# Attention, capacity routing and a cos-MLP on one core: scores in halves of the array's rows, and the float64 pieces moved

## The chip, the cores and the metric

The kernel runs on one core of a Trainium2 chip. The metric is the time of one execution on the device in microseconds (us). Three runs of the kernel before gave a median of 1265.24 us (1261.33 to 1281.06).

## The reference

Three layers follow one another; the output is 1792 x 768 in float32.

```
q_n, k_n = rmsnorm(q, g_q), rmsnorm(k, g_k)          # 4 batches, 12 heads, 448 rows, 64 columns
scores = q_n @ k_n.T / 8;  attn = softmax(scores);  x = attn @ v        # x: 1792 x 768
logits = x @ w_gate                                  # 8 experts, each takes at most 224 tokens
walk over the logits in falling order, give each token to the first expert that has room
out[of e] = relu(x[of e] @ w1[e]) @ w2[e]            # 768 -> 1024 -> 768
h = out @ w_in;  y = (h * cos(h)) @ w_out            # 768 -> 2048 -> 768, w_in and w_out in float64
```

The order of the logits decides which token goes where, so products are kept close to float32: an operand is cut into a high and a low part in the float32r type, and three products (high x high, high x low, low x high) stand for one. The float64 matrices arrive as pairs of 32-bit words and are turned into such parts on the chip.

## The kernel before

The program consists of two plans. A plan (`class Plan`, L51) records each operation with what it reads and writes; `run` (L161) then lists the operations engine by engine, with costs from a table (`cost`, L64) and due times, and that order is fixed in the program. On each engine a step starts in that order. Steps without a successor, as those of the float64 pieces, have the latest due times and fill what is free.

The first plan holds attention and the router's start. Attention goes by pairs of heads, 24 of them (`for P_ in range(NPR)`). For one pair:

- `front` and `turn` (L434) normalise q and k, transpose them with TensorE and cut them into hi and lo parts. For each head these are copied by DMA (`copy`, L366, SP's queue) into a key tile `TK` and a query tile `QS`, so that hi and lo of one head stand on top of each other in the 128 partitions, and a second half `[:, 1]` holds the hi part with one more row: ones for the keys, minus the row maxima for the queries.
- `shifts` (L484) finds the row maxima that keep the exponential in range: seven products s of 128 query rows with all keys, each reduced by VectorE (cm), a transpose, a sign change (cr), and a copy of the row into `QS`. `shift` (L502) does it for the first pair, head by head.
- `scores` (L535) makes, for each of four groups of 112 keys and each head, a score tile in one of two PSUM banks (st): one product over 128 rows (hi and lo of the keys with hi of the queries) and one over 65 rows (hi of the keys with lo of the queries, and the shift). ScalarE writes its exponential to a buffer pf, of which there are `NPF` = 12.
- `weigh` (L553) multiplies the exponentials with v (po: two heads in column halves of the array, float32, two instructions each) and with ones (dn: the sums, in column quarters).
- `rows` (L579) adds the gate logits to the sums' bank by one float32 product of the weighted values with `wg` (32 columns out, 448 columns in), and transposes both by small products with `pick`; VectorE takes the reciprocals of the sums. `tail` (L597) transposes the weighted values for x.

Beside it runs `Narrow.plan` (L254): each of 56 pieces (32 of w_in with 128 x 384 elements, 24 of w_out with 128 x 512) is loaded by SP (nr), turned by ScalarE and VectorE (na, then nr again), and written back to memory by SP. `EARLY` = 36 pieces belong to the first plan, the rest to the second.

The second plan (`moe`) takes the experts in four groups of two. For each expert the router's `phase` picks the next expert and its tokens; for each group the two experts follow, then the cos-MLP on both. The first three phases are the quick ones (`quick`, with count products into rt). The MLP of the first group reads parts that the late pieces have written.

Of the kernel before, what the change touches and what calls it, by code (L numbers as in the profile page):

```python
# [25 lines left out]
class Step:  # L26
    __slots__ = ("ways", "after", "before", "late", "wait", "ready", "end", "eng", "dma", "start", "rush")
# [23 lines left out]
class Plan:  # L51
# [4 lines left out]
    def __init__(self, nc):  # L56
        self.nc, self.steps, self.seen, self.group, self.rush = nc, [], {}, None, 0.0
        self.shared, self.ahead, self.beside = True, 0.0, False
        self.tensor = Engine(self, "PE", nc.tensor)
        self.vector = Engine(self, "DVE", nc.vector)  # L60
        self.scalar = Engine(self, "ACT", nc.scalar)
        self.gpsimd = Engine(self, "POOL", nc.gpsimd)

    def cost(self, eng, name, out, r, kw):  # L64
        n = max([out.free_size()] + [x.free_size() for x in r])
        if eng == "PE":
            if self.key(out)[1]:
                return 0.055
            rhs = r[1] if name == "matmul" else r[0]
            passes = 1 if rhs.dtype != F32 else 4 if name == "matmul" else 2  # L70
            if name == "matmul" and rhs.dtype == F32 and self.beside:
                passes *= {32: 0.32, 64: 0.6}.get(out.partition_size(), 1)
            return max(out.free_size() / 2333.0 + 0.011, 0.107 if rhs.dtype == F32R else 0.0467) * passes
# [28 lines left out]
    def add(self, ways, reads, writes, dma=None):  # L102

        if self.group is not None:
            self.group.append((ways[0], reads, writes))
            return
        s = Step(ways, dma)
        s.rush = self.rush + self.ahead * (ways[0][0] != "DVE")
# [52 lines left out]
    def run(self, order, prefer=0.0, edge=1.0, lag=2.6, hold=0.7, by=6.0, queue=9e9, more=0.0):  # L161
# [21 lines left out]
        free, bus = {}, 0.0  # L183
# [3 lines left out]
        while avail:  # L187
            best = None
            for e in ("PE", "DVE", "ACT", "POOL", "SP"):
# [16 lines left out]
                c = min((g for g in good if g[0] <= t0 + 0.02), key=lambda g: (g[1].late, idx[g[1]]))  # L206
                ahead = [g for g in good if c[0] < g[0] < c[0] + c[2][1] * hold and g[1].late < c[1].late - by]
                if ahead:
                    c = min(ahead, key=lambda g: (g[1].late, idx[g[1]]))
# [19 lines left out]

LEAST = float(np.array([0x38000000], np.uint32).view(np.float32)[0])  # L230
# [53 lines left out]
EPS = 1e-9  # L284
TUNE_A = (3.5, 0.3, 4.5, 0.7, 30.0, 1.2)
NPF = 12
# [8 lines left out]
NHL = 3  # L295
# [15 lines left out]
def attention(tc, P, R, ident, q, k, v, g_q, g_k, w_gate, x_dram, L, other):  # L311
# [4 lines left out]
    with ExitStack() as ctx:  # L316
# [8 lines left out]
        TK = [cst.tile([128, 2, S], F32R, name=f"tk{i}") for i in range(8)]  # L325
        QS = [cst.tile([128, 2, 2, S], F32R, name=f"qs{i}") for i in range(4)]
# [12 lines left out]
        hls = ring("hl", NHL, [128, 2, S], F32R)  # L339
        his = ring("kh", 4, [128, S], F32R)  # L340
        los = ring("kl", 2, [128, S], F32R)
# [59 lines left out]
        for t in TK:  # L401
            zset(t[D:D + 1, 1], 1.0)
# [31 lines left out]
        def turn(P_, i, rs, j):  # L434

            if True:
# [10 lines left out]
                if i:  # L447
                    hi, lo = keys[P_], _ = his(), los()
                else:
                    hl = hls()  # L450
                    hi, lo = hl[:, 0], hl[:, 1]
                if P_ == 0:
                    o = TK[0][0:D, 0] if i else QS[0][0:D, 0, 0]
                    sc.activation(o, p[0:D, :S], AF.Copy, scale=gs[0:D] if i else 1.0)
                if i:
                    sc.activation(hi, p[:, :S], AF.Copy, scale=gs)
                    ve.scalar_tensor_tensor(lo, p[:, :S], gs, hi.bitcast(F32), op0=ALU.mult, op1=ALU.subtract)
                else:
                    sc.activation(hi, p[:, :S], AF.Copy)
                    ve.tensor_tensor(lo, p[:, :S], hi.bitcast(F32), op=ALU.subtract)  # L460
                for h in range(2):
                    r = slice(h * D, (h + 1) * D)
                    if P_ == 0 and h == 0:
                        if i:
                            copy(TK[0][0:D, 1], hi[r])
                            copy(TK[0][D:128, 0], lo[r])
                        else:
                            copy(QS[0][D:128, 0, 0], hl[r, 0])
                            copy(QS[0][0:D, 1, 0], hl[r, 1])
                    elif i:  # L470
                        t = TK[(2 * P_ + h) % 8]
                        copy(t[0:D], hi[r].unsqueeze(1).to_broadcast([D, 2, S]))
                        copy(t[D:128, 0], lo[r])
                    else:
                        t = QS[P_ % 4]
                        copy(t[D:128, 0, h], hl[r, 0])
                        copy(t[0:D, :, h], hl[r])
                    if P_ and not i:
                        z = slice(S - D, S) if h == 0 else slice(0, D)
                        P.either("tensor_copy", mix[P_ % 4][r, r], hi[r, z])  # L480

        keys = {}

        def shifts(P_):  # L484


            cm, t, x = cms(), QS[P_ % 4], 7
            for m in range(x):
                p = b1()[:, :S]
                if m == 3:  # L490
                    w, y = mix[P_ % 4], keys.pop(P_)
# [8 lines left out]
            copy(t[D:D + 1, 1].rearrange("o j s -> o (j s)").rearrange("o (m p) -> o m p", p=128), cr)  # L500

        def shift(P_, heads=(0, 1)):  # L502

            cm, t = cms()[0:CP], QS[P_ % 4]
            K = D if P_ == 0 and heads[0] == 0 else 128
            for h in heads:
                for c in range(NC):
                    p = b1()[0:CP, :S]
                    pe.matmul(p, t[0:K, 0, h, c * CP:(c + 1) * CP], TK[(2 * P_ + h) % 8][0:K, 0], start=True, stop=True)
                    ve.tensor_reduce(cm[:, h * NC + c:h * NC + c + 1], p, AX.X, ALU.max)  # L510
            n, o = len(heads) * NC, heads[0] * NC
            p = bt()[0:n, 0:CP]
            pe.transpose(p, cm[:, o:o + n], ident[0:CP, 0:CP])
            cr = crs()[0:n, 0:CP]
            sc.activation(cr, p, AF.Copy, scale=-1.0)
            row = t[D:D + 1, 1, heads[0]:heads[-1] + 1]
            copy(row.rearrange("o j (c p) -> o (j c) p", c=NC), cr)
# [17 lines left out]
        def scores(P_, a, z):  # L535

            qs = QS[P_ % 4]
            for c in range(a, z):
                sl = slice(c * CP, (c + 1) * CP)
                for h in range(2):  # L540
                    p, tk = bs()[0:CP, :S], TK[(2 * P_ + h) % 8]
# [5 lines left out]
                    block(both)  # L547
                    pf = exps[P_, h, c] = pfs()
                    sc.activation(pf[0:CP], p, AF.Exp)
# [3 lines left out]
        def weigh(P_):  # L553
# [5 lines left out]
            for c in range(NC):  # L559
                def both():  # L560
                    for h in range(2):
                        pe.matmul(po[h * D:(h + 1) * D], t[:, h, c], exps[P_, h, c][0:CP], start=c == 0, stop=c == NC - 1)
# [4 lines left out]
            for h in range(2):  # L567
                def four():
                    for c in range(NC):
                        n = CP + (c == 0)  # L570
                        pe.matmul(pd[32 * c:32 * c + 32], ones[0:n, h], exps.pop((P_, h, c))[0:n], start=h == 0,
                                  stop=h == 1 and c > 0)

                block(four)
# [4 lines left out]
        def rows(y):  # L579
# [3 lines left out]
            block(lambda: pe.matmul(pd[0:32], wg[:, y % NP], outs[y], start=False, stop=True))  # L583
# [3 lines left out]
            for c in range(NC):  # L587
                pe.matmul(p[:, c, 0:18], dn[:, c * CP:(c + 1) * CP], pick[:, 0:18], start=True, stop=True)
# [77 lines left out]
        for P_ in range(min(NPR, AHEAD)):  # L666
# [4 lines left out]
            if P_ == 0:  # L671
                shift(0, (0,))
                shift(0, (1,))
# [20 lines left out]
        P.run(zip(chain, chain[1:]), *TUNE_A)  # L694
# [604 lines left out]
EARLY = 36  # L1299
# [63 lines left out]
```

## Time and profile before

| what | value |
|---|---|
| median of three runs | 1265.24 us |
| the profiled execution: its own time, its span | 1270.09 us, 1268.3 us |
| TensorE, VectorE, ScalarE busy, of the span | 93%, 69%, 52% |
| granted TensorE clock, mean | 0.952 |

The names in the rows: PE is TensorE's products, PEld its weight loads, DVE VectorE, ACT ScalarE, POOL GpSimd, SP the engine whose queue issues most transfers. `st<-qs,tk` is a product that writes a score tile from a query and a key tile; buffer numbers are left out. L47 is the line of the recording helper, so nearly all operations bear it, and the tile names tell them apart. In the timeline, durations of neighbours overlap, because an engine starts the next instruction before the last one has ended; the distance between starts is the cost in a row of instructions. TensorE runs a float32 product as two instructions and a float32r product as one.

### The profile page before, as it was taken

Reading aid. Unit: us, or ns where it says so; the run is one execution under the profiler, and the core shown is the slowest. Engines: PE = TensorE matmul, PEld = TensorE weight load, DVE = VectorE, ACT = ScalarE, POOL = GpSimd, SP = SyncE. Lnnn points to the kernel's source line nnn. Section 1 sums busy time; section 2 is a strip of 40 time slices with the busy share of each in tenths; the row PEclk is TensorE's granted clock in tenths of the full one; section 3 lists DMA queues with packets and bytes.
Section 4 is the critical chain, followed back from the end, with each engine's and each line's share of the span. In section 5 each row is a group of like instructions: output and inputs, shape, how many; then the busy total and the mean of one; then the engine's idle time right before and its main releaser. Section 6 shows DMA issues by size and latency. Waiting matters only on the chain.

```text
span 1268.3 us, 20996 instructions
## 1 busy us (share of the span) xinstructions
PE 1185.7 (93%) x7247; PEld 957.8 (76%) x7247; DVE 873.0 (69%) x2511; ACT 663.8 (52%) x1574; POOL 97.4 (8%) x150
## 2 busy tenths in 40 slices
PE   6999999999985989999789989899999999999996
PEld 4555555555533889788679978789998888999996
DVE  6778768888869878996586569457648737646501
ACT  5577677665654545762454458154538434535500
POOL 4211111111000000000002000000100000100001
PEclk9999899999975789999889999999999999999998
DMA  8888869889754569888867766855776783766762
GB/s 212 193 211 217 207 173 251 227 246 257 232 199 138 154 192 301 282 279 288 288 207 212 216 201 227 239 189 162 225 207 214 234 266 113 223 206 221 244 205 71
DMA packets 201548, 273.52 MB, mean 216 GB/s; under 512 B 16193, under 2 KB 177250, under 8 KB 195298
## 3 DMA queue, kind: packets, MB, share of 16 engines
q1 hardware_dynamic: 198882, 261.17, 69.1%
q0 software_dynamic: 2560, 11.01, 2.9%
q8 instruction: 57, 0.93, 0.3%
q14 instruction: 49, 0.40, 0.1%
HBM read 202.79 MB, written 36.46 MB: 189 GB/s over the span
## 4 chain that ended last, share of the span: by engine, by line
PE 39%; DVE 6%; DMA 6%; ACT 1%; issue 0%; SPq 0%; POOL 0%; POOLq 0%; DVEq 0%; ACTq 0%
PE acc L47 37%; DMA ws<-in_moe_w_dram 2%; DMA AB<-rows 2%; DVE r L47 2%; PE tr L47 1%; DMA wx<-w_in 1%; DVE oh L47 1%; ACT oh L47 1%; PE rt L47 1%; DVE gl L47 1%; DMA nr<-in_moe_w_out_dram 0%; DVE S L47 0%; POOL out_dram L1272 0%; DVE xe L47 0%; DVE ind L47 0%
## 5 line engine op out<-in xcount | busy, mean ns | idle before, releaser
L47 PE MATMUL acc<-gh,wx 128*128 128x224 f32 (+1 forms) x1952 | 376.9, 318 | 0.0
L47 PEld LDWEIGHTS acc<-gh,wx 128*128 128x128 f32 x1952 | 287.3, 195 | 21.3 <-issue 8.6
L47 PE MATMUL acc<-x2h,wx 128*128 128x448 f32 x768 | 228.0, 373 | 0.0
L47 DVE TENSOR_TENSOR wx<-ws,wx 128x768 fp32r<-128x768 f32 (+1 forms) x112 | 119.9, 1070 | 67.0 <-ACT wx L1183 66.8
L47 PEld LDWEIGHTS acc<-x2h,wx 128*128 128x128 f32 x768 | 146.2, 190 | 18.0 <-issue 6.4
L1183 ACT ACTIVATE wx<-ws 128x768 fp32r<-128x768 f32 (+1 forms) x109 | 102.2, 939 | 104.3 <-PE acc L47 73.1
L47 PE MATMUL acc<-gl,wx 128*128 128x448 f32 (+1 forms) x400 | 147.8, 370 | 0.0
L47 PE MATMUL acc<-x2l,wx 128*128 128x448 f32 x384 | 141.6, 369 | 0.0
L47 PE MATMUL acc<-xe,wx 128*128 128x224 f32 x1152 | 136.5, 280 | 0.1
L47 PEld LDWEIGHTS acc<-xe,wx 128*128 128x128 f32 x1152 | 134.5, 196 | 0.5 <-DVE wx L47 0.3
L47 DVE TENSOR_REDUCE cm<-s 128x1 f32<-128x448 f32 (+1 forms) x169 | 99.3, 616 | 43.2 <-PE s L47 42.2
L47 ACT ACTIVATE pf<-st 112x448 f32<-112x448 f32 x192 | 96.0, 540 | 54.8 <-PE st L47 51.4
L47 ACT ACTIVATE oh<-oh 128x896 bf16<-128x896 bf16 x80 | 75.3, 942 | 81.6 <-DVE oh L47 81.5
L47 PE MATMUL st<-qs,tk 128*112 128x448 f32 (+1 forms) x384 | 108.0, 396 | 8.7 <-DMA qs<-cr 7.8
L47 ACT ACTIVATE r<-r 128x448 f32<-128x448 f32 x128 | 73.4, 575 | 42.4 <-DVE r L47 40.9
L47 PE MATMUL po<-pf,vr 112*64 112x448 f32 x384 | 89.7, 580 | 0.0
L47 PEld LDWEIGHTS st<-qs,tk 128*112 128x112 f32 (+1 forms) x384 | 64.1, 182 | 32.1 <-DMA qs<-cr 9.9
L47 DVE TENSOR_SCALAR oh<-AB,b 128x896 bf16<-128x896 f32 x80 | 51.6, 682 | 50.8 <-DMA AB<-rows 50.1
L47 PEld LDWEIGHTS acc<-gl,wx 128*128 128x128 f32 x400 | 78.6, 196 | 5.5
L47 PEld LDWEIGHTS acc<-x2l,wx 128*128 128x128 f32 x384 | 73.0, 190 | 5.3
L1144 POOL DMA_INDIRECT xr<-x,idx x16 | 16.5, 1034 | 694.7 <-issue 215.7
L47 ACT ACTIVATE sq<-qk 112x64 f32<-112x64 f32 (+1 forms) x195 | 57.8, 302 | 20.7 <-DMA qk<-in_q_dram 6.3
(235 smaller groups left out, 1668.7 us busy)
## 6 DMA issues: line engine op xcount, KB each, us to landing
wx<-w_in SPq DMA_DIRECT2D x64, 768.0 KB
wx<-w_out SPq DMA_DIRECT2D x48, 1024.0 KB
ws<-in_moe_w_dram SPq DMA_DIRECT2D x64, 384.0 KB
ws<-in_moe_w_dram SPq DMA_DIRECT2D x48, 512.0 KB
nr<-in_moe_w_in_dram SPq DMA_DIRECT2D x32, 384.0 KB
w_in<-nr SPq DMA_DIRECT2D x32, 384.0 KB
nr<-in_moe_w_out_dram SPq DMA_DIRECT2D x24, 512.0 KB
w_out<-nr SPq DMA_DIRECT2D x24, 512.0 KB
```

Source lines behind the costliest of these rows:

```text
L47: self.plan.add([(self.eng, self.plan.cost(self.eng, name, out, r, kw), lambda: f(*args, **kw))], r, w)
L1144: P.add([("POOL", 1.03, lambda x=x, h=h: nc.gpsimd.indirect_dma_start(out=x, out_offset=None, in_=x_rows, in_offset=bass.IndirectOffsetOnA ...
L1183: P.add([("ACT", 0.093 + n * 0.1067, lambda: nc.scalar.activation(hi, s, AF.Copy)), ("DVE", 0.07 + n * 0.0667, lambda: nc.vector.tensor_co ...
```

## The change

Keys and queries of a pair stay as they leave the transpose, both heads beside each other in the upper and lower 64 partitions, hi and lo in two halves of one tile; the copies go. A score block is made for both heads at once, in four rounds: in each, two products over 64 rows, one for each head, in the upper and the lower half of the array's rows, into the two st banks. The fourth round adds the shift, by a product of a matrix `heads` (a row of ones for each head) with a tile `shift_rows`. `shifts` takes the maxima from the same tiles and serves the first pair too; `shift` goes. The gate product in `rows` is replaced by four products with 18 columns out, which add to the pick products. po is made in two blocks of eight instructions, dn in one. The planner learns the tile form of a product, counts `SWITCH` for a change of form and prefers the form that stands (`SAME`). pf has 18 buffers. `EARLY` is 56: all pieces belong to the first plan.

```diff
-    def run(self, order, prefer=0.0, edge=1.0, lag=2.6, hold=0.7, by=6.0, queue=9e9, more=0.0):
+    def run(self, order, prefer=0.0, edge=1.0, lag=2.6, hold=0.7, by=6.0, queue=9e9, more=0.0,
+            same=0.0):
...
+                def first(g):
+                    return g[1].late - same * (e == "PE" and g[1].mode == mode), idx[g[1]]
...
+            if w[0] == "PE":
+                st += SWITCH * (s.mode != mode)
+                mode = s.mode
...
-NPF = 12
+NPF = 18
...
-        TK = [cst.tile([128, 2, S], F32R, name=f"tk{i}") for i in range(8)]
-        QS = [cst.tile([128, 2, 2, S], F32R, name=f"qs{i}") for i in range(4)]
+        keys = [cst.tile([128, 2, S], F32R, name=f"kk{i}") for i in range(NKQ)]
+        queries = [cst.tile([128, 2, S], F32R, name=f"qq{i}") for i in range(NKQ)]
+        shift_rows = [cst.tile([128, 512], F32R, name=f"sr{i}") for i in range(4)]
+        heads = cst.tile([128, CP], F32R, name="heads")
...
-            for m in range(x):
+            k, q = keys[P_ % NKQ], queries[P_ % NKQ]
+            for m in (0, 4, 1, 5, 2, 6, 3):
                 p = b1()[:, :S]
...
-                    w, y = t[:, 0, h, c:c + 128], TK[(2 * P_ + h) % 8][:, 0]
+                    r = slice(h * D, (h + 1) * D)
+                    w, y = q[r, 0, c:c + 128], k[r, 0]
...
+            for h in range(2):
+                copy(t[h * D:h * D + 1].rearrange("o (m p) -> o m p", p=128), cr[3 * h:3 * h + 4])
...
+                ps = [bs()[0:CP, :S] for h in range(2)]
+
+                def both():
+                    for j in range(4):
+                        for h in range(2):
+                            r = slice(h * D, (h + 1) * D)
+                            w = heads[r] if j == 3 else k[r, j == 1, sl]
+                            y = t[r, h * D:h * D + S] if j == 3 else q[r, int(j == 2)]
+                            pe.matmul(ps[h], w, y, start=j == 0, stop=j == 3)
...
-                    def both():
-                        pe.matmul(p, tk[:, 0, sl], qs[:, 0, h], start=True, stop=False)
-                        pe.matmul(p, tk[0:D + 1, 1, sl], qs[0:D + 1, 1, h], start=False, stop=True)
...
-            block(lambda: pe.matmul(pd[0:32], wg[:, y % NP], outs[y], start=False, stop=True))
...
-                pe.matmul(p[:, c, 0:18], dn[:, c * CP:(c + 1) * CP], pick[:, 0:18], start=True, stop=True)
+                pe.matmul(p[:, c, 0:18], dn[:, sl], pick[:, 0:18], start=True, stop=False)
+                pe.matmul(p[:, c, 0:18], outs[y][:, sl], wg[:, y % NP, 0:18], start=False, stop=True)
...
-EARLY = 36
+EARLY = 56
```

On TensorE, in the middle of attention, the order before reads as follows (st is a score tile, s a product for the maxima, t a transpose, dn with wg the gate product):

```order
L47 MATMUL s_219<-tk_147,qs_152 128x448
L47 MATMUL s_218<-tk_147,qs_152 128x448
L47 MATMUL t_217<-ident,qn_170 128x112 x4
L47 MATMUL st_220<-qs_151,tk_145 112x448 x2
L47 MATMUL st_221<-qs_151,tk_146 112x448 x2
L47 MATMUL dn_223<-xe_203,wg 32x448
L47 MATMUL s_219<-kh_179,mx_185 128x448
```

At a like place the order after reads:

```order
L47 MATMUL st_220<-qq_150,kk_145 112x448
L47 MATMUL st_221<-qq_150,kk_145 112x448
L47 MATMUL st_220<-qq_150,kk_145 112x448
L47 MATMUL st_221<-qq_150,kk_145 112x448
L47 MATMUL st_220<-qq_150,kk_145 112x448
L47 MATMUL st_221<-qq_150,kk_145 112x448
L47 MATMUL st_220<-sr_151,heads 112x448
L47 MATMUL st_221<-sr_151,heads 112x448
L47 MATMUL s_218<-kk_141,qq_146 128x448
L47 MATMUL t_216<-pick,dn_208 112x18
L47 MATMUL t_216<-wg,xe_205 112x18
```

Both st banks are now taken by one block of eight products, a product for the maxima stands alone behind it, and the gate product has become small ones between the pick products.

On VectorE, at the end of attention, the order before has these rows from the last reciprocal on (na and nr are a float64 piece, L and m the router's first steps):

```order
L47 RECIPROCAL r_214<-t_217 112x8
L47 SCALAR_TENSOR_TENSOR na_228<-nr_226,na_228 128x512
L47 TENSOR_TENSOR part<-t_217,r_214 112x4x2x8
L47 TENSOR_SCALAR na_229<-na_229 128x512
L47 TENSOR_REDUCE L<-part 112x32
L47 TENSOR_SCALAR na_229<-na_229 128x512
L47 TENSOR_REDUCE m<-L 112x4
L47 SCALAR_TENSOR_TENSOR na_228<-nr_226,na_228 128x512
```

The order after has, from its last reciprocal on:

```order
L47 RECIPROCAL r_214<-t_216 112x8
L47 TENSOR_TENSOR part<-t_216,r_214 112x4x2x8
L47 TENSOR_REDUCE L<-part 112x32
L47 TENSOR_REDUCE m<-L 112x4
L47 TENSOR_TENSOR oe<-L,m 112x32
```

The pieces have left this place; the last of the 56 now ends ahead of the 23rd reciprocal, and the others stand between the pairs from the first one on (before: two pieces by the third reciprocal, 34 by the 24th; after: six and 56).

## Rows read from the trace of the kernel before

**Rows 1.** The page: the span, and two engines' busy time, share and instructions.

```profile
span 1268.3 us, 20996 instructions
PE 1185.7 (93%) x7247; PEld 957.8 (76%) x7247; DVE 873.0 (69%) x2511; ACT 663.8 (52%) x1574; POOL 97.4 (8%) x150
```

**Rows 2.** Windows: stretch, length, then busy us (instructions) of PE, PEld, DVE, ACT, POOL; clock, DMA.

```profile
25.00:359.00 334.00, 324.72 (x1880) 179.61 (x1878) 266.82 (x746) 220.40 (x694) 46.61 (x42) 0.98 0.83 222
...
377.00:417.00 40.00, 20.09 (x109) 14.70 (x110) 36.07 (x209) 15.97 (x49) 2.29 (x4) 0.53 0.47 142
...
502.00:731.00 229.00, 215.51 (x1322) 195.31 (x1322) 169.08 (x488) 116.08 (x223) 9.88 (x12) 0.96 0.78 256
731.00:939.00 208.00, 200.30 (x1257) 184.36 (x1256) 132.24 (x349) 102.99 (x195) 9.14 (x12) 0.98 0.68 205
939.00:1141.00 202.00, 196.42 (x1256) 181.62 (x1255) 129.54 (x340) 103.14 (x196) 9.14 (x12) 0.99 0.69 211
```

**Rows 3.** Tile t, the reciprocals: duration ns min/median/max, first and last start us.

```profile
L47 DVE RECIPROCAL r<-t x24: 194/200/209, 59.0 to 376.5; 112x8 f32<-112x8 f32 x24
```

**Rows 4.** Timeline of PE within one pair: start us, us, instruction.

```profile
205.46 0.94 PE L47 MATMUL dn<-xe,wg 128*32 128x448 f32 x2
206.33 0.47 PE L47 MATMUL s<-kh,mx 128*128 128x448 f32 x1
206.64 0.37 PE L47 MATMUL s<-tk,qs 128*128 128x448 f32 x1
206.84 0.97 PE L47 MATMUL st<-qs,tk 128*112 128x448 f32 x4
207.65 0.87 PE L47 MATMUL t<-pick,dn 128*112 128x18 f32 x8
208.37 0.66 PE L47 MATMUL s<-tk,qs 128*128 128x448 f32 x2
208.86 0.98 PE L47 MATMUL st<-qs,tk 128*112 128x448 f32 x4
209.77 0.97 PE L47 MATMUL po<-pf,vr 112*64 112x448 f32 x4
210.67 0.28 PE L47 MATMUL t<-ident,cm 128*7 128x128 f32 x1
...
211.27 2.48 PE L47 MATMUL po<-pf,vr 112*64 112x448 f32 x12
213.67 0.47 PE L47 MATMUL s<-tk,qs 128*128 128x448 f32 x1
```

**Rows 5.** Timeline of PE at the start of attention, with the wait before each.

```profile
26.93 0.46 PE L47 MATMUL st<-qs,tk 65*112 65x448 f32 x1 [1.14 <-DMA qs<-cr]
...
36.26 0.46 PE L47 MATMUL st<-qs,tk 65*112 65x448 f32 x1 [2.25 <-DMA qs<-cr]
```

**Rows 6.** Timeline of DVE at the end of attention.

```profile
376.66 0.69 DVE L47 SCALAR_TENSOR_TENSOR na<-nr,na 128x512 int32<-128x512 int32 x1
377.27 0.26 DVE L47 TENSOR_TENSOR part<-t,r 112x64 f32<-112x64 f32 x1
377.41 0.42 DVE L47 TENSOR_SCALAR na<-na 128x512 f32<-128x512 f32 x1
377.74 0.25 DVE L47 TENSOR_REDUCE L<-part 112x32 f32<-112x96 f32 x1
```

**Rows 7.** Groups by form: count, busy us, mean ns of one, idle before.

```profile
L47 DVE SCALAR_TENSOR_TENSOR na<-nr,na 128x384 int32<-128x384 int32 x64 | 35.4, 583 | 0.1
L47 DVE SCALAR_TENSOR_TENSOR na<-nr,na 128x512 int32<-128x512 int32 x48 | 32.6, 685 | 0.1
...
L47 ACT ACTIVATE pf<-st 112x448 f32<-112x448 f32 x192 | 96.0, 540 | 54.8 <-PE st L47 51.4 <-PE dn L47 2.6
```

**Rows 8.** Timeline of PE behind attention's last products, with the wait before it.

```profile
382.82 0.94 PE L47 MATMUL dn<-ab 112*128 112x128 bf16 x4 [6.66 <-DVE ab L47]
```

**Rows 9.** Groups by form of PE from 502 to 731 us: the quick route's count products.

```profile
L47 PE MATMUL rt<-AB 112*128 112x128 bf16 x32 | 5.6, 225 | 1.1 <-ACT AB L47 0.6
...
L47 PE MATMUL rt<-AB 112*128 112x64 bf16 x16 | 2.7, 200 | 0.3
```

More of the change, by code (lines that the diff above doesn't have):

```diff
@@ L26 @@
 class Step:
-    __slots__ = ("ways", "after", "before", "late", "wait", "ready", "end", "eng", "dma", "start", "rush")
+    __slots__ = ("ways", "after", "before", "late", "wait", "ready", "end", "eng", "dma", "start", "rush", "mode")
     def __init__(self, ways, dma):
@@ L57, in __init__ @@
         self.nc, self.steps, self.seen, self.group, self.rush = nc, [], {}, None, 0.0
-        self.shared, self.ahead, self.beside = True, 0.0, False
+        self.shared, self.ahead, self.beside, self.halves = True, 0.0, False, False
         self.tensor = Engine(self, "PE", nc.tensor)
@@ L107, in add @@
         s = Step(ways, dma)
+        s.mode = None
+        if ways[0][0] == "PE" and isinstance(reads[0], bass.AP):
+            w = reads[0]
+            s.mode = (w.partition_size() <= D, 32 if w.free_size() <= 32 else 64 if w.free_size() <= 64 else 128)
         s.rush = self.rush + self.ahead * (ways[0][0] != "DVE")
@@ L182, in run @@
             s.late -= s.rush
-        free, bus = {}, 0.0
+        free, bus, mode = {}, 0.0, None
         avail = [s for s in self.steps if s.wait == 0]
@@ L205, in run @@
                 t0 = min(g[0] for g in good)
-                c = min((g for g in good if g[0] <= t0 + 0.02), key=lambda g: (g[1].late, idx[g[1]]))
-                ahead = [g for g in good if c[0] < g[0] < c[0] + c[2][1] * hold and g[1].late < c[1].late - by]
+                def first(g):
+                    return g[1].late - same * (e == "PE" and g[1].mode == mode), idx[g[1]]
+                c = min((g for g in good if g[0] <= t0 + 0.02), key=first)
+                ahead = [g for g in good if c[0] < g[0] < c[0] + c[2][1] * hold and first(g)[0] < first(c)[0] - by]
                 if ahead:
-                    c = min(ahead, key=lambda g: (g[1].late, idx[g[1]]))
+                    c = min(ahead, key=first)
                 if best is None or c[0] < best[0]:
@@ L400, in attention @@
                 wg[r, :, c], w_gate.rearrange("(e h d) n -> h d e n", h=2, d=D)[h]))], [], [wg[r, :, c]], dma=0.1)
-        for t in TK:
-            zset(t[D:D + 1, 1], 1.0)
+        for t in shift_rows + [heads]:
+            zset(t, 0.0)
+        for h in range(2):
+            zset(heads[h * D:h * D + 1], 1.0)
         zset(ones, 0.0)
@@ L499, in shifts @@
             sc.activation(cr, p, AF.Copy, scale=-1.0)
[L500 to L517, printed above, removed]
+            t = shift_rows[P_ % 4]
+            for h in range(2):
+                copy(t[h * D:h * D + 1].rearrange("o (m p) -> o m p", p=128), cr[3 * h:3 * h + 4])
         vals = {}
@@ L566, in weigh, with fours @@
             P.beside = True
-            for h in range(2):
-                def four():
+            def fours():
+                for h in range(2):
                     for c in range(NC):
                         n = CP + (c == 0)
-                        pe.matmul(pd[32 * c:32 * c + 32], ones[0:n, h], exps.pop((P_, h, c))[0:n], start=h == 0,
-                                  stop=h == 1 and c > 0)
-                block(four)
+                        pe.matmul(pd[32 * c:32 * c + 32], ones[0:n, h], exps.pop((P_, h, c))[0:n], start=h == 0, stop=h == 1)
+            block(fours)
             P.beside = False
@@ L693, in attention @@
         other(P, cst)
-        P.run(zip(chain, chain[1:]), *TUNE_A)
+        P.run(zip(chain, chain[1:]), *TUNE_A, same=SAME)
 CP, NCOL, E, CAP = 112, 16, 8, 224
```

71 lines of the change are left out of this document (26 added, 45 removed).

## Prediction

> **What bounds the kernel now.** I read the page first [rows 1]: TensorE is busy for 93% of the span, VectorE for 69%. Such a mean says nothing about a program with two parts, so next come the stretches [rows 2]. In the attention part, 25 to 359 us, TensorE is busy 324.7 of 334 us and VectorE 266.8; the first is the bound and the second has 67 us to spare. From 377 to 417 us the router runs alone: TensorE is busy half of the time, VectorE 36 of 40. After that TensorE has over 93% in each stretch. The three stretches 502:731, 731:939 and 939:1141 each hold one cos-MLP of a group and the two experts of the next, and take 229, 208 and 202 us: the first, in which the 20 late float64 pieces are turned into parts, is 21 to 27 us longer.
>
> The pace of attention: one reciprocal ends each of the 24 pairs of heads, the first at 59.0, the last at 376.5 us [rows 3]; the mean distance is (376.5 - 59.0) / 23 = 13.8 us. To see what fills a pair I read TensorE's timeline from start to start [rows 4], since the durations overlap. Four score products (st) take 0.81 and 0.91 us; sixteen make 3.5 us a pair. Products for the row maxima (s) take 0.20 to 0.31 us each; the gate product with wg 0.87 us, the eight pick products 0.72 us. For po, four instructions take 0.90 and twelve 2.40 us, hence 0.375 us for one couple of 64-column halves and 0.15 us for leaving that form: 0.90 - 2 x 0.375. A wait plays hardly any part here.
>
> **The change, step by step.** The sum is made against the profiled execution: span 1268.3, own time 1270.1 us, that is 4.9 us above the median of the runs shown (1265.2). I work out a difference and take 4.9 us off at the end.
>
> (a) Scores. Before, a score tile is two products over 128 and 65 rows; after, one block is four rounds of two products over 64 rows, each head in its half of the rows. The columns streamed are the same if both halves run together. No row shows two row halves at once. The nearest row is po: its column halves run together, one couple in 0.375 us, where the gate product without a partner takes 0.87 us for its two instructions [rows 4]. The ends for a round are therefore 0.205 us (a single score product, 0.81 / 4) and 0.41 us (no overlap). I take 0.205, the row of halves being the nearest. Four blocks of four rounds: 3.3 us a pair, for 3.5 before.
>
> (b) Maxima. Six of seven products are now of 64 rows, and couple only where they stand beside each other; in the new order about half do. Fully coupled they would save 0.6 us, alone nothing: I take 0.3.
>
> (c) Gate product. The 0.87 us product goes; four products with 18 columns, eight instructions like the pick ones, come: 0.72. Saved: 0.15.
>
> (d) Form changes. Counted in the order between first and last score product, TensorE changes its tile form 210 times before and 276 times after, though po and dn are in longer runs: the score blocks have become a form of their own, and transposes and pick products stand between them. That is 2.75 more a pair at 0.10 to 0.15 us (0.15 from po; four st before po take 0.10 more than before pick [rows 4]): 0.35 us lost.
>
> Together: 0.2 + 0.3 + 0.15 - 0.35 = 0.3 us a pair less on TensorE, 7 us over 24 pairs; bounds 0 and 15 with full overlap.
>
> (e) Copies. Eight copies of hi and lo parts between partitions in each pair, 192 in all, go from SP's queue; the row of maxima now takes two small ones. Inside the steady part no row shows TensorE held by the large copies, so I cost their removal at nothing there; the 40 transfers of the moved pieces take fewer places on SP's queue than the copies leave. What they do hold is the start: the score products of pair 0 wait for the maxima's copy at 26.93 and again, for the second head, at 36.26 us [rows 5]. After, one chain serves both heads, with seven reductions instead of two chains of four, so the second wait goes and what comes next is VectorE with the same reductions. I take 4 us of the 9.3 between the two as gained; ends 0 and 8.
>
> (f) The 20 float64 pieces. One costs VectorE two shift-and-mask instructions of about 0.60 us from start to start (376.66 to 377.27), two of 0.33 (377.41 to 377.74) and a subtraction priced like the 0.60: 2.46 us [rows 6]; 20 make 49 us. In attention VectorE has 67 us to spare [rows 2], so 18 would be left of 334: 95% busy, in an order fixed beforehand. Spread over the pairs: VectorE's 266.8 us hold 32 narrower pieces, about 2.0 us each by the same rows in the ratio of their means (583 to 685 ns [rows 7]), so 203 us are other work, 8.5 a pair. The new order puts 2.3 pieces in each pair: 8.5 + 2.3 x 2.0 = 13.1 us while the narrow ones last, under TensorE's 13.5; but 8.5 + 2.5 x 2.46 = 14.6 us for the last 9.5 pairs, where the wider ones stand. There VectorE becomes the bound. First part: 14.5 x -0.3 = -4 us. Second: 9.5 x (14.6 - 13.8) = +8 us, or +3 if the instructions pack as in [rows 6], where 0.07 us of each duration overlaps the next. What is queued behind a late reduction is the maxima's transpose, the copy of the shift and then the score block. Steady part of attention: -1 to +4; I take +1, with ends of -15 (TensorE alone decides) and +20 (VectorE with a tenth of idle time).
>
> (g) What the pieces leave behind. At the end of attention the program before still turns two pieces between the last reciprocal and the histogram: TensorE waits there 6.66 us for VectorE [rows 8], of which eight such instructions are about 4.2. After, nothing stands there: -3.5 us. In 502:731 the excess over the two later stretches is 21 to 27 us, of which the quick route, whose 48 count products occur there alone, keeps 8 [rows 9]. That leaves 13 to 19, which I put down to the pieces (49 us of VectorE, and their transfers): -14, ends -5 and -22.
>
> Sum: -4 + 1 - 3.5 - 14 = -20.5. 1270.1 - 20.5 = 1249.6 in the profiled execution's terms; less 4.9: **1245 us**.
>
> The Trainium skill, "TensorEngine Tiling", Key Properties, says that a change of tiling mode drains TensorE. The trace agrees, with the 0.15 us that leaving po's form takes; by that rule the change makes something dearer that the words of it do not name.
>
> **The rivals.**
>
> 1. The halves follow one another. For it: no row shows row halves together. Against it: the column halves overlap fully. A round of 0.41 costs 16 x 0.205 = 3.3 us a pair; a pair takes 16.8 us, VectorE is then no bound, 24 x (16.8 - 13.8) = +72 us in the steady part, and with the other terms 1316 us. This is the slower case; it decides from a round of about 0.27 us on, where what is gained after attention is used up.
>
> 2. They overlap in part. A round needs two weight loads of 112 columns, for which the pick products show 0.09 us apiece (0.72 / 8): 0.18 of a 0.205 us round. If one of the two is not hidden, a round takes 0.295 us, and 384 rounds 35 us more: 1280 us. The Trainium skill, "TensorE: Matmul & The Clock Gate", Part 3 on packing small matmuls, measured 3.07 times for four row tiles together, not four times. Estimated from that page, two halves give 1.54 times, a round 0.27 us and the kernel 1270 us; no run here shows it.
>
> 3. The score block waits for its own exponentials. Before, a tile needs one of two st banks, and the other is free meanwhile; after, a block takes both, and the next block needs both exponentials done: 2 x 0.54 us [rows 7] and the hand-overs, some 1.4 us, in which only other TensorE work can fill. A pair has 13.5 - 3.3 = 10 us of it, but in the new order one gap in four or so holds under 1 us, and VectorE near its limit makes others late. At 1 us a pair, 24 us: 1266 us, no change. Against it: the planner spreads blocks between po, dn and pick.
>
> 4. Attention gains in full: VectorE's instructions pack, (d) costs little, and the score, maxima and start terms reach their ends: -15 - 8 - 4, and 502:731 falls to 205, the mean of the two later stretches, plus the 8 it keeps: -16. 1265 - 43 = 1222 us.
>
> That the pieces are not turned earlier, or that the halves are not made, I leave out: the order shows both.
>
> **How the numbers follow.** The forecast has a chance of 0.48, with its own range 1232 to 1260; rival 1 has 0.08, rival 2 0.08, rival 3 0.19, rival 4 0.17. A measurement of this kernel can tell about 2% from no change, that is below 1240 or above 1290. Faster by that: rival 4 and 0.4 of the forecast's share, 0.36; slower: rival 1, the far end of rival 2, and rival 3 where it adds to a partial overlap, 0.13; within: 0.51. For eight times in ten the range takes in rivals 2, 3 and 4 and stops short of rival 1: 1216 to 1290.
>
> **What would show it.** Right: the two products of a round start within some 10 ns of each other and the rounds 0.2 us apart; the distance of reciprocals is near 13.5 us over the first 14 pairs and 14 or more over the last ten, with VectorE over 93% busy there; the wait before the histogram shrinks to 2 or 3 us; the first stretch of MLP and experts takes 212 to 216 us. Wrong: rounds 0.27 us apart or more (rivals 1 and 2); score blocks on TensorE's list of waits behind the exponentials, tens of us in all (rival 3); TensorE still 97% busy to the end of attention (rival 4); or the stretch after 502 us staying near 229, in which case the pieces were not what made it long.

## The result and the profile after

The changed kernel takes 1249.5 us (median of four runs, 1248.9 to 1252.0) for 1264.3 of the kernel before on the same chip: ratio 0.987, 95% interval 0.983 to 0.992. The profiled execution has a span of 1247.1 us for 1268.3 [rows 1]:

```profile
span 1247.1 us, 21707 instructions
PE 1178.3 (94%) x7773; PEld 959.1 (77%) x7773; DVE 872.1 (70%) x2511; ACT 662.4 (53%) x1572; POOL 96.4 (8%) x155
```

The page says hardly anything: busy shares move by a point. The windows of the changed kernel say more (columns as in [rows 2]):

```profile
25.00:359.00 334.00, 324.93 (x2354) 186.54 (x2352) 316.92 (x864) 244.45 (x748) 45.25 (x43) 0.98 0.61 194
379.00:416.00 37.00, 19.24 (x113) 14.35 (x113) 30.60 (x196) 13.17 (x44) 2.29 (x4) 0.54 0.30 81
499.00:711.00 212.00, 205.85 (x1304) 186.65 (x1303) 133.98 (x409) 100.42 (x195) 9.10 (x12) 0.98 0.63 197
711.00:914.00 203.00, 197.66 (x1255) 182.66 (x1255) 132.22 (x349) 103.09 (x195) 9.13 (x12) 0.98 0.68 210
914.00:1116.00 202.00, 196.56 (x1260) 181.84 (x1259) 131.38 (x347) 103.18 (x195) 9.13 (x12) 0.99 0.68 212
```

In attention VectorE rises from 266.8 to 316.9 us and the DMA share falls from 0.83 to 0.61, though 40 large transfers came in. The first stretch of MLP and experts has lost 35 us of VectorE and 17 us of length. The reciprocals (as in [rows 3]) say where attention stands:

```profile
L47 DVE RECIPROCAL r<-t x24: 197/204/208, 68.1 to 378.5; 112x8 f32<-112x8 f32 x24
```

The first pair ends 9.1 us later than before, the third 10.1 (93.9 for 83.8), the last 2.0. By stage, after less before, in us of the profiled executions (that of the kernel before, at 1270.1 us, lies above its median, so the sum here is larger than the 14.7 us between the medians):

| stage | predicted | measured |
|---|---|---|
| to the third reciprocal | -4 | +10.1 |
| third to last reciprocal | +1 | -8.1 |
| last reciprocal to the first expert's first product | -3.5 | -3.7 |
| from there to the first MLP | 0 | -1.3 |
| first to second MLP | -14 | -13.3 |
| second to third MLP | 0 | -4.6 |
| the rest | 0 | -0.3 |
| sum | -20.5 | -21.2 |

The timeline of TensorE within a pair shows the new blocks (columns as in [rows 4]):

```profile
204.38 1.72 PE L47 MATMUL po<-pf,vr 112*64 112x448 f32 x8
206.03 0.87 PE L47 MATMUL st<-qq,kk 64*112 64x448 f32 x6
206.74 0.37 PE L47 MATMUL st<-sr,heads 64*112 64x448 f32 x2
206.95 0.36 PE L47 MATMUL s<-kk,qq 64*128 64x448 f32 x2
207.24 0.98 PE L47 MATMUL t<-ident,qn 112*128 112x112 f32 x8
```

Eight score products take 0.92 us. The two of a round start 3 or 4 ns apart; the rounds start 0.2 us apart, the second 0.3 us behind the first, because entering the form costs 0.1 us. Two products for the maxima also go as a couple (0.29 us with leaving the form).

And at the start, where the first sums stand behind a block of warm-up products:

```profile
57.49 1.72 PE L47 MATMUL po<-pf,vr 112*64 112x448 f32 x8
59.15 0.47 PE L47 MATMUL s<-kk,mx 128*128 128x448 f32 x1
59.46 4.43 PE L405 MATMUL dn<-ab 112*128 112x256 bf16 x39
63.82 1.71 PE L47 MATMUL dn<-pf,ones 113*32 113x448 f32 x16
```

TensorE's wait before the histogram [rows 8] has shrunk from 6.66 us to 2.81 us:

```profile
381.30 0.94 PE L47 MATMUL dn<-ab 112*128 112x128 bf16 x4 [2.81 <-DVE ab L47]
```

### The profile page after: what moved, and what is told of

It reads as the page before. It is cut to its first block, busy times and chain, and to the rows that moved or that the text cites. A ratio compares the mean times of both kernels' runs of the same rounds, so it can differ in the third digit from the quotient of the medians.

```text
span 1247.1 us, 21707 instructions
## 1 busy us (share of the span) xinstructions
PE 1178.3 (94%) x7773; PEld 959.1 (77%) x7773; DVE 872.1 (70%) x2511; ACT 662.4 (53%) x1572; POOL 96.4 (8%) x155
## 4 chain that ended last, share of the span: by engine, by line
PE 70%; DVE 19%; DMA 7%; ACT 2%; issue 1%; SPq 1%; POOL 0%; POOLq 0%; DVEq 0%; ACTq 0%
PE acc L47 46%; PE st L47 5%; PE po L47 5%; PE t L47 4%; PE dn L47 3%; DMA AB<-rows 2%; DVE r L47 2%; DVE cm L47 2%; PE s L47 2%; PE rt L47 2%; DVE AB L47 2%; DVE na L47 1%; DVE oh L47 1%; PE tr L47 1%; DMA xr<-x,idx 1%
## 5 line engine op out<-in xcount | busy, mean ns | idle before, releaser
L47 PE MATMUL acc<-gh,wx 128*128 128x224 f32 (+1 forms) x1952 | 372.8, 315 | 0.0
L47 PEld LDWEIGHTS acc<-gh,wx 128*128 128x128 f32 x1952 | 283.4, 193 | 17.8 <-issue 6.5
L47 PE MATMUL acc<-gl,wx 128*128 128x448 f32 (+1 forms) x400 | 144.4, 361 | 0.0
L47 PE MATMUL acc<-xe,wx 128*128 128x224 f32 x1152 | 134.0, 277 | 0.6 <-DVE wx L47 0.4
L47 DVE TENSOR_REDUCE cm<-s 128x1 f32<-128x448 f32 x168 | 100.5, 616 | 8.2 <-PE s L47 6.1
L47 PE MATMUL st<-qq,kk 64*112 64x448 f32 x576 | 89.2, 395 | 1.5 <-ACT pf L47 1.5
L47 PE MATMUL po<-pf,vr 112*64 112x448 f32 x384 | 83.1, 552 | 0.0
L47 PEld LDWEIGHTS st<-qq,kk 64*112 64x112 f32 x576 | 47.8, 174 | 39.8 <-issue 15.6
L47 ACT ACTIVATE o<-acc 128x448 f32<-128x448 f32 (+1 forms) x25 | 13.2, 527 | 104.0 <-PE tr L47 81.0
```

What stands on the lines that cost most here:

```text
L47: self.plan.add([(self.eng, self.plan.cost(self.eng, name, out, r, kw), lambda: f(*args, **kw))], r, w)
```

## The experiments

**The pieces and the scores apart.** Two runs give the two missing corners: the changed kernel with the old number of early pieces, and the kernel before with the new one.

```diff
-EARLY = 56
+EARLY = 36
```

> The changed kernel with 36 early pieces instead of 56; 20 pieces go back to the stretch of the first MLP. Theory A (VectorE, 95% busy, sets the pace of attention after the change, and the pieces eat what the score halves gain on TensorE): VectorE falls to about 80% in attention, the distance of reciprocals falls from 13.8 to 13.5 us or less, the last reciprocal comes at 368 to 373 us instead of 378.5, the first stretch of MLP and experts goes back from 211.7 to about 225 us, the wait before the histogram grows by 3 to 4 us; in all 1257 to 1263 us. Theory B (TensorE with its more frequent changes of tile form sets the pace, the pieces cost attention nothing): the last reciprocal stays at 377 to 379 us; in all 1266 to 1269 us.

Measured: 1265.4 us, 0.996 of before (0.9935 to 0.9987). The last reciprocal comes at 373.8 us, between the two theories. VectorE is busy 276.5 of the 320 us from 25 to 345 (304.2 in the changed kernel), yet from the third to the last reciprocal this run takes 282.9 us and the changed kernel 284.7: the 20 pieces cost the steady part of attention 1.8 us, and the rest of the 4.7 us lies ahead of it. The first MLP stretch, from the first MLP to the second, takes 228.6 us (225.0 in the kernel before, 211.7 in the changed one).

```diff
-EARLY = 36
+EARLY = 56
```

> The kernel before with 56 early pieces: the pieces alone are moved, scores and copies stay. Theory A (the score halves are what makes room for the pieces): TensorE at 97% and VectorE at 95% hinder each other, the last reciprocal comes 3 to 10 us later than 376.5, the first stretch of MLP and experts falls from 225 to about 212 us; in all 1250 to 1258 us. Theory B (the halves are worth nothing): the last reciprocal stays at 376 to 379 us and the whole is that of the changed kernel or below, 1245 to 1250 us.

Measured: 1308.0 us, 1.029 (1.024 to 1.033), worse than either theory allowed. The MLP stretch does fall, to 212.6 us, but attention ends 50 us later:

```profile
L47 DVE RECIPROCAL r<-t x24: 188/198/208, 57.0 to 426.4; 112x8 f32<-112x8 f32 x24
```

A window in which it loses much, then the same window of the kernel before and of the changed one:

```profile
206.00:330.00 124.00, 106.10 (x508) 52.90 (x507) 98.14 (x258) 75.95 (x215) 13.27 (x12) 0.87 0.94 260
```

```profile
206.00:330.00 124.00, 121.06 (x702) 66.00 (x701) 105.07 (x300) 78.02 (x217) 17.42 (x15) 1.00 0.88 245
```

```profile
206.00:330.00 124.00, 120.63 (x891) 68.79 (x889) 119.76 (x321) 87.44 (x236) 17.64 (x16) 1.00 0.65 209
```

In the run with copies and 56 pieces no engine is full: TensorE 106 of 124 us, VectorE 98. What is full is the transfers, 0.94. So the moved pieces alone cost 2.9%, the rest of the change alone gains 0.4%, and together they gain 1.3%: the parts can't be added up.

**The copies put back.** In the changed kernel each part of a pair issues its four copies again, into spare buffers, at the place of the instruction that makes lo.

```diff
+                    for o, i in ((u[z], t[r]), (u[r, 0], t[r, 0])):
+                        nc.sync.dma_start(o.bitcast(F32), i.bitcast(F32))
```

> The changed kernel with 184 copies of the removed kind and size put back on SP's queue, into buffers that nobody reads; the order on all other engines is unchanged. Theory D (in the kernel before with 56 pieces it is the copies that get in the way of the pieces' transfers, on SP's queue and on the DMA engines): the DMA share of attention rises from 0.61 to 0.9 or more, pairs of 18 to 28 us appear, the last reciprocal comes 15 to 45 us later than 378.5; in all 1.2 to 3.5% slower than the changed kernel, 1265 to 1295 us. Theory C (that loss came from TensorE's and VectorE's own work or from the order of their instructions): the last reciprocal stays within 4 us, 1249 to 1256 us.

Measured: 1336.4 us, 1.054 (1.049 to 1.060), more than theory D asked for; the last reciprocal at 460.8 us. Its window of attention, then from the list of waits, 100 to 400 us, the two longest of SP's queue and three of ScalarE for transfers (what waits, for what; us, times, longest):

```profile
25.00:345.00 320.00, 276.65 (x1777) 156.37 (x1774) 240.06 (x653) 192.72 (x643) 38.64 (x37) 0.87 0.82 226
```

```profile
SPq L397 <- DVE qq L47: 28.4, 9, 4.7
SPq L282 <- DMA w_in<-nr: 28.3, 12, 4.8
...
ACT na L47 <- DMA nr<-in_moe_w_out_dram: 22.5, 9, 5.9
ACT na L47 <- DMA nr<-in_moe_w_in_dram: 18.7, 6, 5.7
ACT sq L47 <- DMA qk<-in_k_dram: 15.6, 4, 6.8
```

Nobody reads these copies, the order on the four other engines is unchanged, and in attention TensorE, VectorE and ScalarE wait for the copies themselves 0.6 us in all (TensorE's weight loads). So their load on SP's queue and on the DMA engines is the cause. The share reaches 0.82, not the 0.9 expected: a good part is SP's queue itself. L397 is a copy that waits for VectorE, and the loads of q, k and the pieces stand behind it. How much is queue and how much bandwidth stays open. The clock adds to it: the granted clock is 0.87 in this window, 0.98 in the changed kernel, and two of TensorE's longest waits, 4.2 us up to 140.2 and 6.0 us up to 175.6, run into stretches of 6.8 us at half clock, from 138.4 and 172.6.

**VectorE as the bound.** In each of the 20 late pieces four of VectorE's five instructions are left out, nothing else moves.

```diff
+            if i >= 36:
+                for t in plan.steps[was:]:
+                    t.ways = [(t.ways[0][0], t.ways[0][1], lambda: None)]
```

> The changed kernel with four of the five VectorE instructions left out in each of the 20 pieces that the change moved (80 instructions, some 37 us; the values of these parts are therefore not the reference's). Order, transfers and ScalarE's part stay as they are. Theory A (VectorE's load sets the pace where these pieces stand): VectorE falls from 95% to about 85% of attention and the last reciprocal comes 4 to 12 us earlier than 378.5, in all 1237 to 1246 us. Theory B (TensorE sets the pace and VectorE's 95% just fits beside it): the last reciprocal stays within 2 us, 1248 to 1252 us.

```profile
L47 DVE RECIPROCAL r<-t x24: 196/207/208, 68.2 to 378.6; 112x8 f32<-112x8 f32 x24
```

The second half of attention in this run, and in the changed kernel:

```profile
200.00:345.00 145.00, 143.31 (x1044) 81.53 (x1043) 114.83 (x313) 101.61 (x278) 16.90 (x16) 0.99 0.67 212
```

```profile
200.00:345.00 145.00, 141.63 (x1042) 80.90 (x1043) 140.12 (x373) 101.96 (x278) 17.64 (x16) 1.00 0.65 212
```

VectorE falls from 140.1 to 114.8 of 145 us and the last reciprocal does not move: 378.6. Ratio 0.986 (0.981 to 0.990). Theory A falls; TensorE, busy 143 of the 145 us, sets the pace, and VectorE's 97% of this window just fits beside it. The small casts on ScalarE ask the same once more, though here the order changes too:

```diff
-                    P.either("tensor_copy", mix[P_ % 4][r, r], hi[r, slice(S - D, S) if h == 0 else slice(0, D)])
+                    sc.activation(mix[P_ % 4][r, r], hi[r, slice(S - D, S) if h == 0 else slice(0, D)].bitcast(F32), AF.Copy)
```

> The changed kernel with the 48 small casts into mx made by ScalarE instead of VectorE (0.19 us each, 0.64 us where GpSimd works beside them: 14 us of VectorE in all). If VectorE's load sets the pace: VectorE at 91 to 92%, the last reciprocal 2 to 6 us earlier than 378.5, ratio to before 0.982 to 0.986. If not: the last reciprocal within 2 us, ratio 0.986 to 0.989.

Measured: 0.988 (0.984 to 0.992). From 25 to 345 us VectorE has 11 us less (293.5 for 304.2), and nothing is gained. The last reciprocal, at 383.9, is later than either expectation allowed. Between the third and the last, 10.2 us of this run are at half clock, where the changed kernel has none. So the run speaks against VectorE as the bound; which part of its loss is the clock and which the new order, it doesn't part.

**Grouping by form.**

```diff
-SWITCH = 0.15
-SAME = 4.0
+SWITCH = 0.0
+SAME = 0.0
```

> The changed kernel whose planner knows nothing of tile forms (no preference for the form that stands, no price for a change): 308 changes of form between first and last score product instead of 276, and 5 warm-up products instead of 39 ahead of the first pair's sums. Theory A (VectorE sets the pace): steady attention as before the edit within 2 us, the first reciprocal some 4 us earlier, the whole 1244 to 1250 us. Theory B (changes of form on TensorE set the pace): 32 changes at 0.09 to 0.15 us make steady attention 3 to 5 us longer; the whole 1249 to 1255 us.

Measured: 1.009 (1.006 to 1.013), last reciprocal 406.4 us; both theories are far off. The longest pair shows one way in which it comes about. VectorE, GpSimd and TensorE in the same ten microseconds:

```profile
262.65 5.18 DVE L47 SCALAR_TENSOR_TENSOR na<-nr,na 128x384 int32<-128x384 int32 x4
...
262.43 4.99 POOL L47 TENSOR_TENSOR qn<-qk,rs 112x512 f32<-112x512 f32 x4 [35.68 <-DVE rs L47]
...
266.85 0.60 PE L47 MATMUL t<-ident,qn 112*128 112x112 f32 x4
271.07 1.10 PE L47 MATMUL t<-ident,xe 128*112 128x128 f32 x4 [3.62 <-DVE kk L47]
272.10 3.26 PE L47 MATMUL po<-pf,vr 112*64 112x448 f32 x8
```

Four instructions of the pieces take 5.2 us instead of 2.2 (four at the median of 0.55) while GpSimd works; kk behind them is late, TensorE waits 3.6 us, and afterwards po takes 3.3 us instead of 1.7, at a granted clock of 0.5. The same without the late pieces:

> The run without grouping by tile form, and with 36 early pieces; 318 changes of form against 278 in the run with 36 pieces and grouping. Theory V (the 28 us that attention lost without grouping come from VectorE at its limit, whose delays reach TensorE in that order): with VectorE at 85% the loss shrinks to the 40 changes at 0.09 to 0.19 us, 4 to 8 us; last reciprocal 377 to 382 us instead of 373.8, ratio to before 0.998 to 1.003. Theory F (grouping itself carries it, whatever VectorE does): the last reciprocal at 395 us or later, ratio 1.012 or more.

Measured: 1.000 (0.998 to 1.003), last reciprocal 378.2 for 373.8 with grouping. Both lie where theory V put them, but partly because the first reciprocal is 5.6 us earlier (60.1 for 65.7). From the first reciprocal to the last, leaving the grouping out costs 10.0 us with 36 pieces, above V's 4 to 8, and 32.6 us with 56. So some two thirds of the loss are delays that an order with 56 pieces cannot absorb (which of the pieces' loads does it, VectorE's or others', this run doesn't part). The direct worth of the grouping is read from start to start between the third and the 22nd reciprocal, with 36 pieces: the means of s, the qn transposes and the wg products grow by 24, 21 and 10 ns, and all kinds together by some 0.45 us a pair, of which 3.4 us at half clock in this run make 0.1.

**The halves side by side.** The first attempt only changed the order within a block:

```diff
-                    for j in range(4):
-                        for h in range(2):
+                    for h in range(2):
+                        for j in range(4):
```

> The changed kernel with the eight products of a score block in the order of heads: four of the first head, then four of the second, so that only one pair in the middle can stand side by side. If the halves overlap only where their products alternate: a block grows from 0.91 to 1.5 to 1.7 us, 96 blocks add 55 to 75 us to TensorE, the distance of reciprocals grows to 16 us or more, and the whole takes 1295 to 1325 us. If neighbours of any order overlap, or TensorE has that room: under 1260 us.

Measured: 1258.5 us, 0.992 (0.989 to 0.995), last reciprocal 379.8: the second expectation. The block did not grow:

```profile
205.55 0.87 PE L47 MATMUL st<-qq,kk 64*112 64x448 f32 x6
206.26 0.37 PE L47 MATMUL st<-sr,heads 64*112 64x448 f32 x2
206.46 0.37 PE L47 MATMUL s<-kk,qq 64*128 64x448 f32 x2
```

In the trace the products still start in couples, here 1 to 13 ns apart (median of all blocks 14, for 4 in the changed kernel), and in 83 of 94 blocks the two shift products come last together: three products of the second head pass the first head's shift product, which stands ahead of them in the program. So this run doesn't price the overlap. The second attempt makes them unable to overlap, by a product over all rows at the end of each head:

```diff
-                            w = heads[r] if j == 3 else k[r, j == 1, sl]
-                            y = t[r, h * D:h * D + S] if j == 3 else q[r, int(j == 2)]
+                            w = only[h] if j == 3 else k[r, j == 1, sl]
+                            y = t[:, h * D:h * D + S] if j == 3 else q[r, int(j == 2)]
```

> The changed kernel with the fourth product of a score block made over all 128 rows (a matrix with a row of ones for one head alone), head after head, so that the halves cannot stand side by side; same number of products, same columns, same results. If the overlap of the halves is what carries the score block: a block takes 1.6 to 1.9 us instead of 0.91, 96 blocks add 65 to 95 us to TensorE, pairs take 16.5 to 17.5 us, in all 1310 to 1345 us. If TensorE has room because VectorE sets the pace: a block still takes 1.6 us or more, but the whole grows by less than 25 us, to 1275 at the most.

Far worse than expected: 1558 us (median; the fastest run 1533.5, before 1266.4). One block at full clock, and one at half (0.50 granted, the lower of the clock's two levels, 1.2 of 2.4 GHz):

```profile
136.36 0.86 PE L47 MATMUL st<-qq,kk 64*112 64x448 f32 x3
137.16 0.46 PE L47 MATMUL st<-sr,only 128*112 128x448 f32 x1
137.55 0.86 PE L47 MATMUL st<-qq,kk 64*112 64x448 f32 x3
138.34 0.46 PE L47 MATMUL st<-sr,only 128*112 128x448 f32 x1
138.73 0.46 PE L47 MATMUL s<-kk,qq 64*128 64x448 f32 x1
...
141.11 1.44 PE L47 MATMUL st<-qq,kk 64*112 64x448 f32 x3
142.47 0.71 PE L47 MATMUL st<-sr,only 128*112 128x448 f32 x1
```

2.37 us for 0.92: eight products at 0.2 and four changes of form with 0.77 us together, 0.19 each. 96 blocks make 140 us. The other 145 to 170, over the changed kernel, go with the clock: by their mean clocks (0.842 and 0.964) some 490 us of this execution ran at half clock and some 90 of the changed kernel's. From 100 to 200 us the mean fell to 0.70 with TensorE busy all the time:

```profile
100.00:200.00 100.00, 100.00 (x384) 50.03 (x384) 49.03 (x132) 45.22 (x138) 7.48 (x7) 0.70 0.33 106
```

**The start.** The warm-up products write the bank of the first pair's sums, so these wait until all 150 are through.

```diff
-WARM = 150
+WARM = 105
```

> The changed kernel with 105 warm-up products instead of 150; the 39 that stood as one block ahead of the first pair's sums go. If these warm-ups are what delays the start: the first reciprocal comes at 62 to 65 us instead of 68.1, the third at 88 to 91 instead of 93.9, and the last some 3 to 5 us earlier than 378.5; 1244 to 1248 us. If VectorE, filled by the first pieces and the maxima, sets the start: the first reciprocal is earlier, but the third stays at 93 to 95 and the last within 2 us; 1248 to 1252 us.

Measured: 1249.5 us; the third reciprocal comes at 84.1 us, as before the change (83.8):

```profile
L47 DVE RECIPROCAL r<-t x24: 197/202/210, 58.9 to 372.1; 112x8 f32<-112x8 f32 x24
```

Attention is 6.4 us shorter, more than expected. Behind it the profiled execution loses 7.7 us again against the changed kernel's, 3.9 of them from the third MLP to the fourth; why is open. The whole, 0.984 (0.980 to 0.989), can't be told from the changed kernel's 0.987. With the first pieces held back as well:

```diff
+        for s in [s for s in P.steps[n:] if s.ways[0][0] == "ACT"][0:3:2]:
+            s.after[ends[HELD]] = True
```

> As the run with 105 warm-up products, and the first two pieces are not turned before the first reciprocal, so that VectorE's first 70 us belong to the maxima alone. If VectorE's early pieces hold the start: the third reciprocal comes at 83 to 88 us, the last 4 to 8 us earlier than 378.5 if the pieces still fit (they do by count, the last before the 24th pair); 1241 to 1247 us. If the single chain of maxima with its products at half clock is what holds it: the third reciprocal stays at 92 to 95 us and the whole within 2 us of the run with 105 alone.

Measured: third reciprocal 88.4, 4.3 us later than without holding them, last 380.9, ratio 0.990 (0.985 to 0.995). There is no gain: the early pieces are not what holds the start. And with the casts on ScalarE:

> The casts on ScalarE and 105 warm-up products together. If both gains hold: first reciprocal at 58 to 62 us, the last at 368 to 373, ratio to before 0.977 to 0.983, the best so far. If attention's gains are lost again behind it: the last reciprocal early, but the ratio 0.984 to 0.989.

Measured: first reciprocal 60.1, last 374.4; 1246.0 us, 0.980 (0.976 to 0.984), beside 1257.2 for the same kernel with 150 warm-ups on the same chip. The warm-ups are worth 0.8% there. This is the fastest of all, but its interval still overlaps that of the changed kernel.

## Why the prediction was right, and where its steps were not

The time (1245, measured 1249.5) and the sum (-20.5, measured -21.2) were right; some of the steps below them were not, and that the sum came so near is in part luck. The 4.5 us between the two times are the 4.9 that the prediction took off for the profiled execution before: that of the changed kernel, 1248.9 us, does not lie above its median.

(a) Scores: the halves overlap fully, rounds 0.2 us apart; rivals 1 and 2 are out, and the run without overlap gives the price. The gain of 0.2 us a pair did not come: from start to start (mean of each kind between the third and the 22nd reciprocal, times its count in a pair), scores cost 3.89 us a pair for 3.80 before, since each block now also pays for a form of its own (the 0.1 us at its first round, and the leaving).

(b) and (d) held, (c) came to a third. Per pair, from the same sums: maxima -0.37 (predicted -0.3), gate product with pick -0.05 (-0.15), po -0.09; the three kinds of transposes, which now follow a change of form, +0.38 (the predicted price of the changes was 0.35). All in all -0.04 us a pair where -0.3 was predicted for (a) to (d): TensorE's work is unchanged.

(e) failed twice. "I take 4 us of the 9.3 between the two as gained": the second copy's wait did go, but what was late next was neither VectorE nor the maxima, it was the warm-up products. The first sums wait for their bank and start at 63.82 us, in the run with 105 warm-ups at 52.25; the block of 39 takes 4.4 us of that, the rest is other products that the order put ahead. The step looked at waits and not at what the new order had put in front. Nor were the 4 us there without the warm-ups: the third reciprocal then comes at 84.1 us, 83.8 before the change. And "I cost their removal at nothing there" put a term at nothing without a test. From 50 to 350 us of the kernel before, TensorE's longest waits are for the copy of the maxima's row, which stands on the same queue as the large copies (what waits, for what; us, times, longest):

```profile
PE st L47 <- DMA qs<-cr: 4.4, 3, 1.7
```

The changed kernel, with such row copies but without the large ones, has no wait for one there. That the large copies held the row back was not tested on its own. And the removal is what makes room for the pieces; the copies put back cost 82 us of attention.

(f) failed in its mechanism. "There VectorE becomes the bound": it is 97% busy from 200 to 345 us, as predicted, and bounds nothing. The last nine distances of reciprocals, 258.4 to 378.5 us, are 13.3 us in the mean (11.1 to 16.5), not 14; the first fourteen are 13.6. The steady part gained 8.1 us, mostly a thing of the clock: before, 20.4 us of it ran at half clock, as these two of its windows show, after none of it (clock 1.00 from 93.9 to 378.5):

```profile
150.80:157.60 6.80, 6.80 (x23) 4.32 (x21) 5.74 (x21) 4.13 (x15) 1.04 (x1) 0.50 0.66 158
359.00:372.60 13.60, 13.24 (x36) 4.56 (x36) 7.16 (x23) 5.49 (x11) 0.00 (x0) 0.50 0.81 285
```

Work takes 1.7 times as long there (three score products 1.36 us for 0.80 from start to start in the run without overlap), so the 20.4 us at half clock cost some 8 us, by estimate: the whole gain. The first of the two stretches follows on the longest wait for the row copy, 1.69 us up to 149.13. The higher clock is no chance of one execution: it is 0.963 or 0.964 in the four runs of the changed kernel, and 0.953 to 0.956 in the median of the kernel before on each of three chips. That the copies' removal brings it is argued, not shown.

Start and steady part, wrong by +14 and -9, nearly cancel: that is the luck in the sum. The -4.6 us of the stretch from the second MLP to the third were not predicted and stay open; with the same 56 pieces that stretch takes 200.8 to 206.1 us over the runs.

(g) held: -3.7 and -13.3 us. Every run with 56 early pieces, the one on the kernel before too, has 211 to 215 us in the first MLP stretch; with 36 the kernel before has 225.0 and both runs of the changed kernel 228.6.

Rival 3 is out: score products wait 1.5 us in all for exponentials. (By its own terms, 1245 and 24, its time would have been 1269, not 1266; nothing hangs on it.) Rival 4 was half right. Its sign is there: TensorE is busy 141.6 of the 145 us from 200 to 345 and sets the pace. Its gain is not: attention ends 2.0 us later than before, and only the MLP stretch came near its figure.

## What to carry to other kernels

Two edits that each look neutral or bad can be the condition for one another: here the copies had to leave SP's queue before the pieces could enter it, so each edit is to be tried with and without the other. A busy share of 97% is no proof of a bound; leaving work out in an unchanged order tests it. And where a planner writes the order, look at what stands in front of the first result, warm-up work too.

## What was not expected of the hardware

- Products in the two row halves pass each other: written head after head they still ran side by side (in couples 14 ns apart in the median). The Trainium skill, "TensorEngine Tiling (Array Packing)", Key Properties, says that tiles operate independently; the run agrees.
- With the score products on half of the rows one after another, the granted clock was 0.71 in the window from 25 to 345 us, where the changed kernel has 0.98, with TensorE 99% busy. Whether the half rows or the four changes of form in each block bring it down, the run doesn't part.
- Some of VectorE's instructions that touch SBUF alone stretch while GpSimd multiplies: the cast into mx takes 0.19 us alone and 0.64 beside it (medians of the changed kernel, 37 and 11 of them). Not all do: one of the pieces' 128 x 512 instructions beside GpSimd kept its 0.68 us, and reductions from PSUM keep 0.61 us.
